# Wider weight blocks, and attention and the second layer nearer to their users, in a fused attention and two-layer kernel

## Chip, cores and metric

The kernel runs on one core of a Trainium2 chip. The metric is the time of one execution in microseconds (us) on the device; it is given as the median of several runs. One further execution was taken with the hardware profiler, and all rows of a profile below come from that one. TensorE is called PE in the profile, VectorE DVE, ScalarE ACT, GpSimd POOL and SyncE SP.

## What is computed

Pooled attention, and two feed-forward layers on its result, all in float32:

```python
def _attn_ref(q, kv, w_sr):                    # q: 1 x 12288 x 128, kv: 1 x 384 x 32 x 128
    kv_pool = kv.reshape(B, H // r, r, W // r, r, C).mean(axis=(2, 4))    # r = 4: 768 keys
    k = v = kv_pool.reshape(B, -1, C) @ w_sr
    s = (1.0 / np.sqrt(C)) * (q @ k.transpose(0, 2, 1))
    a = np.exp(s - s.max(-1, keepdims=True))
    a /= a.sum(-1, keepdims=True) + 1e-09
    return a @ v
def _moe_ref(x, w_in, w_out):                  # d_model 128, d_ff 2048
    h = x @ w_in
    return np.where(h > 0.0, h, np.exp(np.minimum(h, 0.0)) - 1.0) @ w_out
def _moe2_ref(x, w_in, w_out):
    h = x @ w_in
    return np.maximum(0.01 * h, h) @ w_out
# _moe2_ref(_moe_ref(attention of all 12288 rows))
```

Weights are handed in as 64-bit floats, as two 32-bit words each.

## The kernel before

**Tiling.** The 12288 rows are 24 chunks of 512. Every product is made of three matmuls on a high and a low part of each operand (`mm3`, lines 87 to 89), so that it keeps nearly float32 accuracy. Of a chunk, attention has four tiles of 128 rows (L347 to L426): scores against 768 keys into PSUM, the negated maximum on DVE (L351, `largest`), exp on ACT (L358), the inverse of the sum (L366, L367) and a scaling on POOL (L377). From chunk 2 on a tile is then sent through DRAM and fetched again in another order, transposed on DVE (L406, `turn`) and split into a high part on ACT (L422) and a low part on DVE (L426, the tail). Eighteen matmuls with v (L437, `values`) give the chunk's input of layer 1, split into xh on ACT (L441) and xl on DVE (L445).

**Units.** Of a chunk, each layer has 8 units, each of 256 of the 2048 hidden columns: 6 matmuls up into a PSUM place, the activation, and 6 matmuls down into the chunk's accumulator py. Layer 1's unit costs ACT two operations (L472, L475), DVE two (L479 and the tail L499) and POOL one (L485); layer 2's costs ACT two (L491, L495) and DVE one (L499). The output of layer 1 is split into x2h (ACT, L515) and x2l (DVE, L519), layer 2's input. The list `units` (L454 to L459) alternates a unit of layer 1 and one of layer 2, with layer 2 behind by D2 units of its kind: 12 units of layer 1 alone come first, and 12 of layer 2 alone come last. A unit's place in this list is its number n; the first unit is n = 0.

**Weights.** Each of the four matrices is brought in in blocks of WP = 256 hidden columns, 32 blocks in all. A block is loaded by SP into one of WS = 4 slots `ws` (L167). Then it is turned from 64-bit words into a high and a low float32 part (`w_parts`, L183): Abs of the upper words on ACT (L195), bounds on POOL (L199), on DVE a shift (L205), the sign (L212), the power (L219) and the lower words by that power (L229), on ACT the high part (L225); on PE three products with unit matrices, the rest (L236 to L238, of which the first, with a float32 operand, runs as two passes), and on ACT the low part (L241). The temporaries m, a and b of a block are one set out of two, held from Abs to the rest.

**Order.** A planner in the kernel's own text writes out the order of the instructions on every engine before the program runs (L535 to L807). Every `step` has an engine, an assumed length, the steps it follows and a key in units of n. Repeatedly the step is taken that can begin first by the assumed times; among those that can begin at once, the one with the lowest key. A step whose key is over 12 above the lowest open one is not yet looked at. `take` and `give` keep count of buffers: three PSUM places for scores, ups, rests and values together, the slots ws, the sets wt and others. On the chip each engine then runs its list in that order, and waits on semaphores where a real time differs from an assumed one.

The keys around the change: a chunk's attention from chunk 2 on starts at base = (n of its first layer-1 unit) - AHEAD, with 4 between its tiles; chunk 0 starts at -14 and chunk 1 at -8 with 2 between its tiles (L596). The maximum of a tile is at +0.5, its turn at +5.5, its tail at +6.5; with end the key of the last tile, values are at end + 7.5 and xl at end + 9.2. Layer 1's down of unit n is at n + 4, x2l at 0.4 behind the last down. A weight block is due 6 ahead of the first unit that uses it (L562, L563), and its load another 8 earlier. All ups keep the order of n (`chain["up"]`, L665).

Of the kernel before, what the change touches and what calls it, by code (L numbers as in the profile page):

```python
# [10 lines left out]
F32 = mybir.dt.float32  # L11
F32R = mybir.dt.float32r
U32 = mybir.dt.uint32
AF = mybir.ActivationFunctionType
# [4 lines left out]
P = 128  # L19
CH = 512  # L20
S = 32
WP = 256
WS = 4
D2 = 12
NEARLY = 2


LAG = {1: 4, 2: 4}
AHEAD = 28
SPACE = 4  # L30
WAHEAD = 6
REACH = 12
# [7 lines left out]
def pooled_attention_elu_leaky_kernel(  # L40
# [20 lines left out]
    nc = tc.nc  # L61
# [21 lines left out]
    def f(ap):  # L83
        return ap.bitcast(F32)
# [6 lines left out]
    def pool(name, bufs, **kw):  # L91
        return ctx.enter_context(tc.tile_pool(name=name, bufs=bufs, **kw))
# [25 lines left out]
    d_p = pool("scratch", 4, space=bass.MemoryType.DRAM)  # L118
    xs_p = pool("xs", 2)
    ws_p = pool("ws", WS)  # L120
    wt_p = pool("wt", 2)
    ps_p = [pool(f"ps_{i}", 1, space=PSUM) for i in range(3)]
    ps_y = pool("ps_y", 2, space=PSUM)

# [40 lines left out]
    wst, wt, w_ps = {}, {}, {}  # L165
# [17 lines left out]
    def w_parts(i):  # L183

        k, p = wjobs[i]
        pp, o = divmod(p * WP, CH)
        hi, lo = w_hi[k, pp][:, o:o + WP], w_lo[k, pp][:, o:o + WP]  # L190
        u = lambda x: x.bitcast(U32)

        def w_abs():
            wt[i] = [wt_p.tile([P, WP], t, tag=x, name=x) for x, t in zip("mab", (F32, F32, F32R))]
            nc.scalar.activation(out=wt[i][0], in_=f(wst[i][:, :, 1]), func=AF.Abs)  # L195

        def w_bound():
            m, a, b = wt[i]
            nc.gpsimd.tensor_scalar(  # L199
                out=m, in0=m, scalar1=TOP, scalar2=LEAST, op0=ALU.min, op1=ALU.max  # L200
            )

        def w_shift():
            m, a, b = wt[i]
            nc.vector.tensor_scalar(  # L205
                out=u(a), in0=u(m), scalar1=3, scalar2=0x3FFFFFF8,
                op0=ALU.logical_shift_left, op1=ALU.bitwise_and,
            )

        def w_sign():  # L210
            m, a, b = wt[i]
            nc.vector.scalar_tensor_tensor(  # L212
                out=u(a), in0=wst[i][:, :, 1], scalar=0xC0000000, in1=u(a),
                op0=ALU.bitwise_and, op1=ALU.bitwise_or,
            )

        def w_power():
            m, a, b = wt[i]
            nc.vector.tensor_scalar(  # L219
                out=u(m), in0=u(a), scalar1=0xFF800000, scalar2=None, op0=ALU.bitwise_and  # L220
            )

        def w_head():
            m, a, b = wt[i]
            nc.scalar.activation(out=hi, in_=a, func=AF.Copy)  # L225

        def w_b():
            m, a, b = wt[i]
            nc.vector.scalar_tensor_tensor(  # L229
                out=b, in0=wst[i][:, :, 0], scalar=2.0 ** -52, in1=m, op0=ALU.mult, op1=ALU.mult  # L230
            )

        def w_rest():
            m, a, b = wt[i]
            ps = w_ps[i][:, 0, :WP]
            nc.tensor.matmul(ps, ident, a, start=True, stop=False)  # L236
            nc.tensor.matmul(ps, minus, hi, start=False, stop=False)
            nc.tensor.matmul(ps, plus, b, start=False, stop=True)  # L238

        def w_tail():  # L240
            nc.scalar.activation(out=lo, in_=w_ps.pop(i)[:, 0, :WP], func=AF.Copy)  # L241

        return w_abs, w_bound, w_shift, w_sign, w_power, w_head, w_b, w_rest, w_tail

    with tc.tile_pool(name="kvp", bufs=1) as kvp, tc.tile_pool(name="sums", bufs=2) as sum_p:
# [7 lines left out]
        for i in range(WS):  # L255
# [9 lines left out]
            out=red,  # L265
            in_=ident.rearrange("p (h r w) -> p h w r", h=4, r=R),
# [4 lines left out]
            out=pool_m[:, 96:128],  # L271
# [231 lines left out]
    def down(n, i):  # L503
        m, c, u = units[n]
        if u == 0 and i == 0:
            yps[m, c] = ps_y.tile([P, CH], F32, tag="y", name="py")
        wh, wl = wblk(f"o{m}", 2 * u + i)
        mm3(
            yps[m, c], wh, wl, gh_u[n][:, i, :], gl_u[n][:, i, :],
            u == 0 and i == 0, u == NU - 1 and i == 1,  # L510
        )
# [26 lines left out]
    def step(engine, length, do, after, key):  # L538
        steps.append((engine, length, do, [a for a in after if a is not None], key))
        return len(steps) - 1  # L540

    def take(i, pool, n, bufs, put=None):

        takes.setdefault(i, []).append((pool, n, bufs, put))

    def give(i, pool, n):
        gives.setdefault(i, []).append((pool, n))

    PE, DVE, ACT, POOL, SP = range(5)
    where = {}  # L550
# [7 lines left out]
    w_ready = {}  # L558
    w_ends = []
    for i, (k, p) in enumerate(wjobs):  # L560
        m = int(k[1])
        n = where[m, 0, p] + (0 if k[0] == "i" else LAG[m])  # L562
        key = n - WAHEAD  # L563
        ld = None
        if i >= WS:
            ld = step(SP, 0.4, lambda i=i: load_w(i), [], key - 8)
            take(ld, "ws", i, WS)
        steps_w = w_parts(i)
        ab = step(ACT, 0.4, steps_w[0], [ld], key)
        bo = step(POOL, 0.5, steps_w[1], [ab], key)  # L570
        sh = step(DVE, 0.25, steps_w[2], [bo], key + 0.1)
        si = step(DVE, 0.4, steps_w[3], [sh], key + 0.2)
        po = step(DVE, 0.25, steps_w[4], [si], key + 0.3)
        hd = step(ACT, 0.4, steps_w[5], [si], key + 0.2)
        wb = step(DVE, 0.4, steps_w[6], [po], key + 0.4)
        wr = step(PE, 0.8, steps_w[7], [hd, wb], key + 0.5)
        take(wr, "ps", None, 3, lambda ps, i=i: w_ps.__setitem__(i, ps))
        wl = step(ACT, 0.45, steps_w[8], [wr], key + 0.6)
        give(wl, "ps", wr)
        take(ab, "wt", i, 2)  # L580
        give(wr, "wt", i)
        give(wb, "ws", i)
        w_ready[k, p] = wl


    x_ready = {}
# [7 lines left out]
    for c in range(NCH):  # L594
# [5 lines left out]
        for j in range(NJ):  # L600
            t = c * NJ + j
            key = base + gap * j
            after = [q_ready[c], last_sc]
# [34 lines left out]
        if c + 1 < NCH:  # L638
            ld = None
            if c + 1 >= 2:  # L640
                ld = step(SP, 2.2, lambda c=c: load_q(c + 1), [], end - 8)
# [20 lines left out]

    chain = dict.fromkeys(("up", "act", "tail", "down"))
    for n, (m, c, u) in enumerate(units):
        after = [w_ready[f"i{m}", u], x_ready[m, c], chain["up"]]  # L665
        u0 = step(PE, 0.69, lambda n=n: up(n, 0), after, n)
        u1 = chain["up"] = step(PE, 0.69, lambda n=n: up(n, 1), [u0], n)
        take(u0, "ps", None, 3, lambda ps, n=n: ps_u.__setitem__(n, ps))
        if m == 1:
            re = step(ACT, 0.95, lambda n=n: relu(n), [u1, chain["act"]], n + 0.5)  # L670
            xe = step(ACT, 1.05, lambda n=n: elu_exp(n), [re], n + 0.5)
            el = step(DVE, 1.3, lambda n=n: elu(n), [xe], n + 1)
            gh = step(POOL, 1.1, lambda n=n: elu_head(n), [el], n + 1.5)
            chain["act"] = re
            take(re, "r", n, 2)
            give(el, "r", n)
            take(el, "g", n, 3)
            take(gh, "gh", n, 4)
            give(el, "ps", u0)
            both = [el, gh]  # L680
        else:
            lh = step(ACT, 0.95, lambda n=n: leaky_head(n), [u1, chain["act"]], n + 0.5)
            lk = step(ACT, 0.95, lambda n=n: leaky(n), [lh], n + 0.5)
            chain["act"] = lk
            take(lh, "gh", n, 4)
            take(lk, "g", n, 3)
            give(lk, "ps", u0)
            both = [lh, lk]
        tl = chain["tail"] = step(DVE, 1.25, lambda n=n: tail(n), [*both, chain["tail"]], n + 2)
        take(tl, "gl", n, 3)  # L690
        give(tl, "g", n)
        d0 = step(
            PE, 0.69, lambda n=n: down(n, 0), [tl, w_ready[f"o{m}", u], chain["down"]],
            n + LAG[m],
        )
        d1 = chain["down"] = step(PE, 0.69, lambda n=n: down(n, 1), [d0], n + LAG[m])
        if u == 0:
            take(d0, "py", (m, c), 2)
        give(d1, "gl", n)
        give(d1, "gh", n)  # L700
        if u == NU - 1 and m == 1:
            hx = step(ACT, 0.55, lambda c=c: head_x2(c), [d1], n + LAG[m] + 0.3)
            x_ready[2, c] = step(DVE, 0.72, lambda c=c: tail_x2(c), [hx], n + LAG[m] + 0.4)
            take(hx, "x2", c, 2)
            give(x_ready[2, c], "py", (m, c))
        elif u == NU - 1:
            ty = step(DVE, 0.75, lambda c=c: turn_y(c), [d1], n + LAG[m] + 2)
            take(ty, "y", c, 1)
            give(ty, "py", (m, c))
            st = step(SP, 2.2, lambda c=c: store(c), [ty], n + LAG[m] + 3)  # L710
            give(st, "y", c)
        if u == NU - 1:
            give(u1, "xs" if m == 1 else "x2", c)
# [124 lines left out]
```

## Time and profile before

| | |
|---|---|
| median of 3 runs | 1362.68 us (1359.66 to 1364.47) |
| the profiled execution | 1353.33 us |
| its span, first to last instruction | 1351.5 us |
| busy: PE, DVE, ACT, POOL | 97%, 82%, 74%, 29% of the span |
| mean granted clock of TensorE | 0.994 of full speed |

Busy time of PE is modelled: matmuls overlap, and one of 512 columns shows about 0.39 us while the next one starts 0.23 us later. A PE that is busy all the time is therefore not proof of full use, but a PE that is idle is proof of a loss. The clock is given as a share of 2.4 GHz; it has two levels, 1.2 and 2.4 GHz, so that a mean of 0.85 says that 30% of the stretch ran at the lower one.

### The profile page before, as it was taken

What the parts mean: (1) busy time and instruction counts of PE and PEld (TensorE: products, weight loads), DVE (VectorE), ACT (ScalarE), POOL (GpSimd) and SP (SyncE); (2) the same over time, 40 slices, a digit from 0 to 9 for tenths busy, and PEclk for the clock granted to TensorE, in tenths of its full rate; (3) what the DMA queues carried; (4) which work ended last, traced back from release to release, by engine and by line L of the source; (5) the groups of instructions that cost most, each with busy time, mean ns of one, the idle gap of its engine ahead of it and who ended that gap; (6) DMA issues with size and microseconds to landing.
All of it is one profiled execution on the core that took longest, in us unless ns stands there. A gap on an engine that the chain in (4) does not pass through costs nothing.

```text
span 1351.5 us, 16631 instructions
## 1 busy us (share of the span) xinstructions
PE 1311.3 (97%) x5864; PEld 1085.9 (80%) x5864; DVE 1114.8 (82%) x1335; ACT 1000.0 (74%) x1245; POOL 385.7 (29%) x326
## 2 busy tenths in 40 slices
PE   5788999999999999999999999999999999999998
PEld 5576778888888888888888888888888888888886
DVE  6889998898887887887887888978878878887664
ACT  2666877778777786787777777777877867777775
POOL 0344432332332332322323323222323323231110
PEclk8999999999999999999999999999999999999999
DMA  8133322312322223223223123122222232220001
GB/s 250 56 109 118 113 63 73 81 54 69 82 67 64 79 62 79 70 64 86 70 63 86 59 63 86 59 63 80 65 75 72 61 87 71 55 78 24 8 8 16
DMA packets 170659, 97.63 MB, mean 72 GB/s; under 512 B 104912, under 2 KB 154192, under 8 KB 170576
## 3 DMA queue, kind: packets, MB, share of 16 engines
q1 hardware_dynamic: 169376, 96.36, 25.5%
q8 instruction: 47, 0.77, 0.2%
q10 hardware_dynamic: 1200, 0.20, 0.1%
q14 instruction: 36, 0.29, 0.1%
HBM read 55.64 MB, written 40.89 MB: 71 GB/s over the span
## 4 chain that ended last, share of the span: by engine, by line
PE 89%; DVE 6%; ACT 2%; issue 1%; POOL 1%; DMA 0%; SPq 0%; DVEq 0%; POOLq 0%; ACTq 0%
PE ps L88 15%; PE ps L87 15%; PE ps L89 15%; PE py L88 12%; PE py L89 12%; PE py L87 12%; PE ps L437 6%; DVE gl L499 1%; DVE a L212 1%; DVE g L479 1%; DVE el L426 1%; PE ps L236 1%; DVE nm L351 1%; DVE a L205 0%; DVE e L406 0%
## 5 line engine op out<-in xcount | busy, mean ns | idle before, releaser
L499 DVE TENSOR_TENSOR gl<-g,gh 128x1024 fp32r<-128x1024 f32 x384 | 470.2, 1253 | 94.5 <-POOL gh L485 76.8
L485 POOL TENSOR_SCALAR gh<-g 128x1024 fp32r<-128x1024 f32 x192 | 222.8, 1160 | 668.6 <-DVE g L479 632.4
L88 PE MATMUL py<-gl,wh_o 128*128 128x512 f32 x768 | 302.3, 394 | 2.3 <-DVE gl L499 2.2
L89 PE MATMUL py<-gh,wl_o 128*128 128x512 f32 x768 | 301.1, 392 | 0.0
L87 PE MATMUL py<-gh,wh_o 128*128 128x512 f32 x768 | 299.9, 390 | 0.2 <-DVE x2l L519 0.2
L472 ACT ACTIVATE r<-ps 128x1024 f32<-128x1024 f32 x192 | 197.0, 1026 | 138.7 <-PE ps L89 138.5
L479 DVE SCALAR_TENSOR_TENSOR g<-r,ps 128x1024 f32<-128x1024 f32 x192 | 232.9, 1213 | 72.7 <-ACT r L475 72.3
L491 ACT ACTIVATE gh<-ps 128x1024 fp32r<-128x1024 f32 x192 | 196.5, 1023 | 58.3 <-PE ps L89 58.3
L475 ACT ACTIVATE r<-r 128x1024 f32<-128x1024 f32 x192 | 203.8, 1062 | 5.8
L495 ACT ACTIVATE g<-ps 128x1024 f32<-128x1024 f32 x192 | 196.0, 1021 | 0.0
L377 POOL TENSOR_SCALAR e<-e,rs 128x768 f32<-128x768 f32 x88 | 135.3, 1538 | 172.7 <-DVE rs L367 127.8
L88 PEld LDWEIGHTS py<-gl,wh_o 128*128 128x128 f32 x768 | 144.2, 188 | 32.4 <-DVE gl L499 4.5
L89 PEld LDWEIGHTS py<-gh,wl_o 128*128 128x128 f32 x768 | 144.3, 188 | 30.6
L87 PEld LDWEIGHTS py<-gh,wh_o 128*128 128x128 f32 x768 | 144.3, 188 | 29.1 <-issue 0.4
L87 PE MATMUL ps<-xh,wh_i 128*128 128x512 f32 x384 | 151.1, 393 | 1.0 <-ACT e L358 1.0
L88 PE MATMUL ps<-xl,wh_i 128*128 128x512 f32 x384 | 151.6, 395 | 0.0
L89 PE MATMUL ps<-xh,wl_i 128*128 128x512 f32 x384 | 151.0, 393 | 0.0
L88 PE MATMUL ps<-x2l,wh_i 128*128 128x512 f32 x384 | 150.7, 392 | 0.0
L89 PE MATMUL ps<-x2h,wl_i 128*128 128x512 f32 x384 | 150.3, 391 | 0.0
L87 PE MATMUL ps<-x2h,wh_i 128*128 128x512 f32 x384 | 150.0, 391 | 0.0
L358 ACT ACTIVATE e<-ps,nm 128x768 f32<-128x768 f32 x96 | 85.9, 895 | 33.4 <-DVE nm L351 31.1
L426 DVE TENSOR_TENSOR el<-e,eh 128x768 fp32r<-128x768 f32 x88 | 99.1, 1126 | 7.5 <-ACT eh L422 7.4
(80 smaller groups left out, 1628.4 us busy)
## 6 DMA issues: line engine op xcount, KB each, us to landing
d<-e SPq DMA_DIRECT2D x88, 384.0 KB, 2.6
x<-d SPq DMA_DIRECT2D x88, 384.0 KB, 3.0
qn<-in_q_dram SPq DMA_DIRECT2D x96, 64.0 KB, 2.4
kv<-in_kv_dram SPq DMA_DIRECT2D x12, 512.0 KB, 8.7
out_dram<-y SPq DMA_DIRECT2D x94, 64.0 KB, 2.2
ws<-in_moe_w_in_dram SPq DMA_DIRECT2D x16, 256.0 KB, 2.9
ws<-in_moe_w_out_dram SPq DMA_DIRECT2D x16, 256.0 KB, 2.7
out_dram<-y ACTq DMA_DIRECT2D x2, 64.0 KB, 2.9
```

What stands on the lines that cost most here:

```text
L87: nc.tensor.matmul(ps, w_hi, x_hi, start=start, stop=False)
L88: nc.tensor.matmul(ps, w_hi, x_lo, start=False, stop=False)
L89: nc.tensor.matmul(ps, w_lo, x_hi, start=False, stop=stop)
L377: nc.gpsimd.tensor_scalar(out=x, in0=e, scalar1=rs_t.pop(t), scalar2=1.0, op0=ALU.mult, op1=ALU.mult)
L426: nc.vector.tensor_tensor(out=lo, in0=e_t.pop(t), in1=f(hi), op=ALU.subtract)
L472: nc.scalar.activation(out=r_u[n], in_=ps_u[n], func=AF.Relu, scale=-1.0)
L475: nc.scalar.activation(out=r_u[n], in_=r_u[n], func=AF.Exp, scale=-1.0)
L479: nc.vector.scalar_tensor_tensor(out=g_u[n], in0=r_u.pop(n), scalar=-1.0, in1=ps_u.pop(n), op0=ALU.add, op1=ALU.max)
L485: nc.gpsimd.tensor_scalar(out=gh_u[n], in0=g_u[n], scalar1=1.0, scalar2=0.0, op0=ALU.mult, op1=ALU.add)
L491: nc.scalar.activation(out=gh_u[n], in_=ps_u[n], func=AF.Prelu, alpha=0.01)
L495: nc.scalar.activation(out=g_u[n], in_=ps_u.pop(n), func=AF.Prelu, alpha=0.01)
L499: nc.vector.tensor_tensor(out=gl_u[n], in0=g_u.pop(n), in1=f(gh_u[n]), op=ALU.subtract)
```

## The change

Weight blocks become 512 columns wide, so there are 16 of them, in two slots for four. The temporaries m, a and b become three buffers of their own, one of each, taken and given back one by one: m from Abs to the last DVE step, a from the shift to the rest, b from that last DVE step to the rest. The assumed lengths of the weights' steps grow. Attention from chunk 2 on starts 24 units ahead of its chunk, in place of 28, and layer 2 runs 10 units behind layer 1, in place of 12. A block is due by the first unit that uses any of its columns. The diff, without the lines that only unpack m, a and b differently:

```diff
-WP = 256
-WS = 4
-D2 = 12
+WP = 512
+WS = 2
+D2 = 10
...
-AHEAD = 28
+AHEAD = 24
...
-    wt_p = pool("wt", 2)
+    wt_p = pool("wt", 1)
...
         def w_abs():
-            wt[i] = [wt_p.tile([P, WP], t, tag=x, name=x) for x, t in zip("mab", (F32, F32, F32R))]
-            nc.scalar.activation(out=wt[i][0], in_=f(wst[i][:, :, 1]), func=AF.Abs)
+            wt[i] = {"m": wt_p.tile([P, WP], F32, tag="m", name="m")}
+            nc.scalar.activation(out=wt[i]["m"], in_=f(wst[i][:, :, 1]), func=AF.Abs)
...
         def w_shift():
-            m, a, b = wt[i]
+            m, a = wt[i]["m"], wt_p.tile([P, WP], F32, tag="a", name="a")
+            wt[i]["a"] = a
...
         def w_b():
-            m, a, b = wt[i]
+            m, b = wt[i]["m"], wt_p.tile([P, WP], F32R, tag="b", name="b")
+            wt[i]["b"] = b
...
-        n = where[m, 0, p] + (0 if k[0] == "i" else LAG[m])
+        n = where[m, 0, p * WP // (2 * P)] + (0 if k[0] == "i" else LAG[m])
...
-        ab = step(ACT, 0.4, steps_w[0], [ld], key)
-        bo = step(POOL, 0.5, steps_w[1], [ab], key)
-        sh = step(DVE, 0.25, steps_w[2], [bo], key + 0.1)
-        si = step(DVE, 0.4, steps_w[3], [sh], key + 0.2)
-        po = step(DVE, 0.25, steps_w[4], [si], key + 0.3)
-        hd = step(ACT, 0.4, steps_w[5], [si], key + 0.2)
-        wb = step(DVE, 0.4, steps_w[6], [po], key + 0.4)
-        wr = step(PE, 0.8, steps_w[7], [hd, wb], key + 0.5)
+        ab = step(ACT, 0.65, steps_w[0], [ld], key)
+        bo = step(POOL, 1.0, steps_w[1], [ab], key)
+        sh = step(DVE, 0.6, steps_w[2], [bo], key + 0.1)
+        si = step(DVE, 0.7, steps_w[3], [sh], key + 0.2)
+        po = step(DVE, 0.6, steps_w[4], [si], key + 0.3)
+        hd = step(ACT, 0.65, steps_w[5], [si], key + 0.2)
+        wb = step(DVE, 0.7, steps_w[6], [po], key + 0.4)
+        wr = step(PE, 0.9, steps_w[7], [hd, wb], key + 0.5)
         take(wr, "ps", None, 3, lambda ps, i=i: w_ps.__setitem__(i, ps))
-        wl = step(ACT, 0.45, steps_w[8], [wr], key + 0.6)
+        wl = step(ACT, 0.65, steps_w[8], [wr], key + 0.6)
         give(wl, "ps", wr)
-        take(ab, "wt", i, 2)
-        give(wr, "wt", i)
+        for tag, begun, over in (("m", ab, wb), ("a", sh, wr), ("b", wb, wr)):
+            take(begun, tag, i, 1)
+            give(over, tag, i)
...
-        after = [w_ready[f"i{m}", u], x_ready[m, c], chain["up"]]
+        after = [w_ready[f"i{m}", 2 * P * u // WP], x_ready[m, c], chain["up"]]
...
-            PE, 0.69, lambda n=n: down(n, 0), [tl, w_ready[f"o{m}", u], chain["down"]],
+            PE, 0.69, lambda n=n: down(n, 0), [tl, w_ready[f"o{m}", 2 * P * u // WP], chain["down"]],
```

## Rows read from the trace of the kernel before

**Rows 1.** The page: busy us of each engine (share of the span), instructions.
```profile
PE 1311.3 (97%) x5864; PEld 1085.9 (80%) x5864; DVE 1114.8 (82%) x1335; ACT 1000.0 (74%) x1245; POOL 385.7 (29%) x326
```
**Rows 2.** Windows: stretch, length, busy PE, PEld, DVE, ACT, POOL; clock, DMA share, GB/s.
```profile
30.00:66.50 36.50, 26.80 (x148) 22.33 (x148) 32.83 (x73) 23.47 (x51) 11.93 (x16) 1.00 0.21 59
66.50:90.00 23.50, 19.39 (x76) 15.26 (x76) 18.38 (x31) 15.64 (x27) 10.60 (x12) 0.85 0.34 112
90.00:112.50 22.50, 19.42 (x91) 15.38 (x90) 21.75 (x37) 15.28 (x29) 7.46 (x9) 1.00 0.44 122
112.50:130.00 17.50, 14.98 (x65) 11.59 (x64) 17.26 (x23) 13.52 (x20) 10.29 (x8) 1.00 0.31 99
130.00:200.00 70.00, 68.66 (x312) 55.52 (x311) 68.48 (x112) 54.54 (x91) 30.28 (x26) 1.00 0.28 87
252.00:304.00 52.00, 52.00 (x234) 43.35 (x233) 43.84 (x50) 39.74 (x48) 15.31 (x12) 1.00 0.26 70
```
**Rows 3.** Groups, whole span: instruction xcount | busy us, mean ns | idle before, releasers.
```profile
L377 POOL TENSOR_SCALAR e<-e,rs 128x768 f32<-128x768 f32 x88 | 135.3, 1538 | 172.7 <-DVE rs L367 127.8 <-ACT x2h L515 37.5 <-issue 2.4
...
L212 DVE SCALAR_TENSOR_TENSOR a<-ws,a 128x256 uint32<-128x256 uint32 x32 | 19.2, 612 | 0.7
...
L229 DVE SCALAR_TENSOR_TENSOR b<-ws,m 128x256 fp32r<-128x256 uint32 x32 | 13.6, 440 | 2.0 <-DVE m L219 0.5
...
L205 DVE TENSOR_SCALAR a<-m 128x256 uint32<-128x256 uint32 x32 | 11.1, 360 | 3.2 <-POOL m L199 2.8 <-PE ps L238 0.5
...
L219 DVE TENSOR_SCALAR m<-a 128x256 uint32<-128x256 uint32 x32 | 10.1, 330 | 0.6
...
L284 DVE TENSOR_TENSOR s<-kv 128x512 f32<-128x512 f32 x12 | 8.3, 689 | 5.8 <-DMA kv<-in_kv_dram 5.4
```
**Rows 4.** Single lines: duration ns min/median/max, first and last start us, shape.
```profile
L212 DVE SCALAR_TENSOR_TENSOR a<-ws,a x32: 409/426/1267, 36.2 to 186.6; 128x256 uint32<-128x256 uint32 x32
...
L205 DVE TENSOR_SCALAR a<-m x32: 250/286/1157, 30.8 to 186.2; 128x256 uint32<-128x256 uint32 x32
```
**Rows 5.** PE in order of time: start, us, instruction [idle before]; up to unit 0.
```profile
64.91 0.70 PE L236 MATMUL ps<-a,ident 128*128 128x256 f32 x2 [2.30 <-ACT e L358]
...
66.57 0.63 PE L87 MATMUL ps<-xh,wh_i 128*128 128x512 f32 x1
```
**Rows 6.** DVE and PE in order of time, around units 8 and 11.
```profile
111.40 0.68 DVE L445 TENSOR_TENSOR xl<-ps,xh 128x512 fp32r<-128x512 f32 x1
...
112.48 0.40 PE L87 MATMUL ps<-xh,wh_i 128*128 128x512 f32 x1
...
124.74 0.40 PE L87 MATMUL ps<-xh,wh_i 128*128 128x512 f32 x1
...
131.52 0.68 DVE L519 TENSOR_TENSOR x2l<-py,x2h 128x512 fp32r<-128x512 f32 x1
```
**Rows 7.** Groups of DVE from 66.5 to 112.5 us.
```profile
L212 DVE SCALAR_TENSOR_TENSOR a<-ws,a 128x256 uint32<-128x256 uint32 x10 | 6.4, 636 | 0.3
...
L406 DVE STREAM_TRANSPOSE e<-x 128x768 f32<-128x768 f32 x3 | 2.9, 971 | 0.0
...
L426 DVE TENSOR_TENSOR el<-e,eh 128x768 fp32r<-128x768 f32 x3 | 2.9, 952 | 0.1
```
**Rows 8.** DVE and PE in order of time: chunk 8's xl, x2l and first readers.
```profile
460.07 0.69 DVE L445 TENSOR_TENSOR xl<-ps,xh 128x512 fp32r<-128x512 f32 x1 [1.05 <-ACT xh L441]
...
483.35 0.39 PE L87 MATMUL ps<-xh,wh_i 128*128 128x512 f32 x1
...
544.86 0.68 DVE L519 TENSOR_TENSOR x2l<-py,x2h 128x512 fp32r<-128x512 f32 x1
...
566.74 0.39 PE L87 MATMUL ps<-x2h,wh_i 128*128 128x512 f32 x1
```
**Rows 9.** DVE and PE in order of time: the last chunk's x2l and first reader.
```profile
1316.23 0.68 DVE L519 TENSOR_TENSOR x2l<-py,x2h 128x512 fp32r<-128x512 f32 x1
...
1319.79 0.39 PE L87 MATMUL ps<-x2h,wh_i 128*128 128x512 f32 x1
```

More of the change, by code (lines that the diff above doesn't have):

```diff
@@ L193, in w_abs @@
         def w_abs():
-            wt[i] = [wt_p.tile([P, WP], t, tag=x, name=x) for x, t in zip("mab", (F32, F32, F32R))]
-            nc.scalar.activation(out=wt[i][0], in_=f(wst[i][:, :, 1]), func=AF.Abs)
+            wt[i] = {"m": wt_p.tile([P, WP], F32, tag="m", name="m")}
+            nc.scalar.activation(out=wt[i]["m"], in_=f(wst[i][:, :, 1]), func=AF.Abs)
         def w_bound():
-            m, a, b = wt[i]
+            m = wt[i]["m"]
             nc.gpsimd.tensor_scalar(
@@ L210, in w_sign @@
         def w_sign():
-            m, a, b = wt[i]
+            m, a = wt[i]["m"], wt[i]["a"]
             nc.vector.scalar_tensor_tensor(
@@ L217, in w_power @@
         def w_power():
-            m, a, b = wt[i]
+            m, a = wt[i]["m"], wt[i]["a"]
             nc.vector.tensor_scalar(
@@ L223, in w_head @@
         def w_head():
-            m, a, b = wt[i]
+            a = wt[i]["a"]
             nc.scalar.activation(out=hi, in_=a, func=AF.Copy)
         def w_b():
-            m, a, b = wt[i]
+            m, b = wt[i]["m"], wt_p.tile([P, WP], F32R, tag="b", name="b")
+            wt[i]["b"] = b
             nc.vector.scalar_tensor_tensor(
@@ L233, in w_rest @@
         def w_rest():
-            m, a, b = wt[i]
+            a, b = wt[i]["a"], wt[i]["b"]
             ps = w_ps[i][:, 0, :WP]
```

## The prediction

> **What bounds the kernel now.** I read the page's busy times first, then the windows by stretch, then the groups of DVE, and last single instructions in order of time. PE is busy for 97% of the span [rows 1], but that is a mean over two regimes. Later on (252 to 304 us) PE fills its 52 us completely at the full clock, and DVE has 8.2 us of 52 to spare [rows 2]: there a step taken from DVE or ACT is worth nothing. The other regime is the fill, 30 to 200 us. In its five stretches PE stands idle for 9.7, 4.1, 3.1, 2.5 and 1.3 us (length less PE's busy time), 20.7 us in all, and from 66.5 to 90 the mean granted clock is 0.85, which costs 0.15 x 23.5 = 3.5 us more [rows 2]. So about 24 us is all that a reordering of the fill can win, since PE's own work stays. In the same stretches DVE is busy for 32.8 of 36.5, 18.4 of 23.5, 21.8 of 22.5, 17.3 of 17.5 and 68.5 of 70 us: from 90 us on DVE sets the pace; from 66.5 to 90 it has 5 us free, and chains through several engines do.
>
> **Wider weight blocks.** Of each block DVE runs four operations. Their totals are 19.2, 13.6, 11.1 and 10.1 us, 54.0 us in 32 blocks, 1.69 a block [rows 3]. Sixteen blocks of 512 columns take their place. The two-input operations, 0.426 us undisturbed (median of L212 [rows 4]), go to the 0.689 us of L284, which has two inputs of 512 columns [rows 3]. For the two TENSOR_SCALARs no row has 512 columns. They take 0.286 us for 256 (median of L205 [rows 4]), so at 512 between that and twice that, 0.57; I take 0.42, the middle, since columns cost them less than the two-input ones. A block then costs 2 x 0.69 + 2 x 0.42 = 2.2 us undisturbed.
>
> The second unknown is what a disturbed one costs. L212 has a median of 426 ns and a longest of 1267 [rows 4] at a mean of 612 [rows 3], so some of the 32 wait for something. An undisturbed narrow block is 2 x 0.426 + 2 x 0.286 = 1.42 us, so 0.27 us a block is such waiting; after the change it is between 0.27 (as much per instruction) and 0.54 (as much per column). I take 0.3: 2.5 us a block, 40 us in all, and DVE has 14 us less to do over the whole fill. The bounds are 6 us (0.57 and 0.54) and 18 us (0.286 and 0.27).
> The Trainium skill (SBUF — State Buffer, section Who interferes with whom) says that a VectorE instruction with two SBUF inputs and a reading GpSimd instruction exclude each other for a whole instruction, whichever began first. By that the wait is what is left of POOL's instruction, however wide DVE's own is, and the sum would be the one with 0.27; a mean of 1538 ns for POOL's L377 beside the longest L212 of 1267 [rows 3, 4] agrees.
>
> ACT's three operations a block shrink likewise, but ACT is busy for only 54.5 of 70 us and less before [rows 2], so I cost that at nothing; its own idle time hides it. PE's rests: two narrow ones took 1.66 us from the first one's start to the first unit's [rows 5], and one wide one streams the same columns: nothing. The loads move the same bytes, in 16 transfers for 32 and through two slots for four. They lie on SP's queue with the sends and fetches of attention, whose result has over 20 us to spare now (below). The four loads ahead of the loop become two of twice the size; the weights' first step on DVE comes only at 31 us and the first unit at 66.6 [rows 4, 5], so that is free too, and without that cover would cost one transfer's time.
>
> **Attention later.** A chunk's keys start 24 units ahead of its first unit, and D2 = 10 puts chunk 2's first unit at 22 for 20. So chunk 2's four score tiles get keys -2, 2, 6, 10 for -8, -4, 0, 4. Two of them now go ahead of the first unit. PE's last wait there, 2.30 us for the exp of one of them, goes: -2.3 us (bounds 0, if a rest waits for something else, and -4.0, if half of the slow clock behind it goes too, 1.7 of 3.5) [rows 2, 5]. The first unit then starts near 64.
>
> From the first unit to the ninth (66.6 to 112.5) the limit is chunk 1's xl: it ends at 112.1, and the ninth unit's first matmul starts at 112.5 [rows 6]. xl has key 7.2 (end -2 and 9.2), and DVE work with a lower key goes first. By keys, 9 wide blocks stand before it where 17 narrow ones did; in this stretch there were 9.5 narrow ones (L212 has 10, [rows 7]), and 5 wide ones will be: 9.5 x 1.69 - 5 x 2.5 = 3.6 us less. Of attention it had three turns and three tails, 2.9 us each [rows 7]. One tile of chunk 2 gets as far by key 7.2, so two of each go, 3.9 us, and a maximum comes in, no longer than a tail, 0.95: 2.9 us less. Together that is 6.5 us of DVE. From 90 to 112.5 DVE is busy 97%, and a saved us is a us; from 66.5 to 90 it is busy 78% [rows 2]. I take three quarters: -4.9 us (bounds 0 and -6.5). One score tile that PE had done by then, about 1 us, moves behind the ninth unit into a stretch with little idle: +1.0 us (bounds 0 and 2).
>
> From 112.5 to 200 PE is idle for 3.8 us [rows 2]. Seven wide blocks for fifteen narrow ones are 7.9 us less for DVE, against attention that comes later: -1 us (bounds 0 and -3).
>
> In the steady part the cover shrinks but lasts. A chunk's xl ends at 460.8 and is read at 483.4, 22.6 us later; its layer 2 starts 25 units on, at 566.7, so a unit is 3.34 us [rows 8], and four units less leave 9.2 us. Nothing that stands behind attention on DVE, ACT or SP is due before xl. Nothing; if that cover went, every chunk would pay.
>
> **The second layer two units earlier.** In the steady part layer 2 of a chunk starts 2 x D2 - 13 units after the end of its layer 1: 7 for 11. x2l ends at 545.5 and is read at 566.7, 21.2 us later [rows 8]; less 13.4 leaves 7.8: nothing. At the start layer 2's first unit becomes the twelfth, in place of the fourteenth. Now x2l of chunk 0 runs from 131.5 to 132.2 while the twelfth unit starts at 124.7 [rows 6]: 7.5 us too late as things stand. But DVE has less to do before it: 20 x 1.69 - 11 x 2.5 = 6.3 us of weights, two tiles of chunk 2 with their maximum, turn and tail (some 5.7 us, by [rows 7]) and the two operations of one unit, near 2.4 us: 14.4 us in all, so x2l ends near 118, and the twelfth unit, 6.2 us earlier by the terms above, comes at 118.5. I take 0 (bounds 0 and +7.5). At the end, x2l of the last chunk is ready 2.9 us before its reader [rows 9], with five units of layer 2 between it and layer 1's last up; there will be three. The last down can move up, since fewer units stand ahead of it: +0.5 us (bounds 0 and +2).
>
> **The sum.** -2.3 - 4.9 + 1.0 - 1.0 + 0 + 0.5 = -6.7 us. The profiled execution took 1353.33 us (span 1351.5 and 1.8 around it) and would take 1346.6. The median of the runs shown, 1362.68, is 9.35 us above it, so there it is 1356. A difference under 0.3%, 4 us, can't be told from none for this kernel.
>
> **The rivals.**
> - One set of temporaries holds the blocks up. The shift of a block can't start before the rest of the block ahead has run on PE, and its Abs not before that block's last DVE step. With two sets one such wait of the shift shows, 0.5 us [rows 3]. Unit work queued on DVE behind the shift waits too, and PE for that. At 0.8 us, half of what two narrow rests take, for the nine blocks ahead of the ninth unit it is 7 us, all of the gain: 1363. For it speaks DVE's full load; against it, that ten narrow blocks were spread over 46 us, so a wide one has some 9 us, more than its own 2.5 of DVE and 1.7 of PE. Chance 0.22.
> The Trainium skill (Trainium Kernel Development and Optimization, section Best Practices) asks for double buffers so that DMA and compute overlap, which speaks against single ones in general; no run here shows yet what they cost.
> - The slower one: layer 2's first up meets its x2l in DVE's backlog, and, since all ups keep one order, the layer-1 units behind it wait as well. Place: the twelfth unit. Price: 7.5 us with the backlog as it is, of which PE fills 2.3 with work that the earlier first unit released, and 0.5 at the end: +5.7 us, 1368. It ends above the time before if DVE's work ahead of x2l shrinks by less than 5.7 us, not 14.4. For it: DVE is busy for 17.3 of the 17.5 us before 130 [rows 2]. Against it: x2l's key, 11.4, is below those of the units that follow. Chance 0.16.
> - The whole saving counts, and half the slow clock goes: -4.0 - 6.5 - 3.0 + 1.0 = -12.5 us: 1350. Chance 0.12.
> - My forecast, 1352 to 1358: 0.50.
>
> **How the numbers follow.** Faster by over 0.3%: forecast and whole saving, 0.62. Same: 0.22. Slower: 0.16. The range runs from the whole saving, less the 3 us by which the lowest run lies under the median, to two thirds of the way into the slower rival: 1347 to 1366.
>
> **What would show it.** The first matmul on xh near 64, with no wait of 2 us for an exp before it; the ninth unit near 105; L205 and L212 16 times, at 0.4 and 0.7 us; PE idle for under 16 us between 30 and 200; xl some 9 us ahead of its reader in the steady part and no idle there; x2l of chunk 0 near 118. Wrong would be: DVE's shift waiting for PE's rests, PE waiting for x2l at the twelfth unit, or any wait of PE after 200 us.

## The result, and the profile after

| | before | after |
|---|---|---|
| median of the executions taken with the prediction | 1363.58 us (4, from 1359.66 to 1364.91) | 1347.76 us (4, from 1346.46 to 1349.57) |
| ratio, 95% interval | | 0.9903 (0.9876 to 0.9929) |
| the profiled execution | 1353.33 us | 1346.46 us |
| its span | 1351.5 us | 1344.5 us |

The changed kernel is faster by about 1%; the forecast was 1356 in a range from 1347 to 1366. The two comparisons don't agree: by the medians the gain is 15.8 us, by the two profiled executions 6.9 us, and the forecast had 6.7. Most of what follows is about that gap.

The windows of after, in the stretches of [rows 2] and with the same columns (stretch, length, busy time and instructions of PE, PEld, DVE, ACT and POOL, clock, DMA):

```profile
30.00:66.50 36.50, 27.40 (x138) 20.99 (x138) 29.55 (x54) 24.10 (x41) 12.56 (x13) 1.00 0.20 51
66.50:90.00 23.50, 20.13 (x74) 14.37 (x75) 21.81 (x32) 17.04 (x26) 9.68 (x9) 0.93 0.50 157
90.00:112.50 22.50, 21.23 (x88) 15.64 (x87) 20.24 (x25) 15.72 (x22) 9.08 (x8) 1.00 0.35 106
112.50:130.00 17.50, 15.40 (x61) 10.49 (x61) 17.07 (x22) 10.53 (x15) 7.07 (x5) 1.00 0.24 56
130.00:200.00 70.00, 67.94 (x290) 53.82 (x289) 63.14 (x77) 56.69 (x73) 23.10 (x19) 1.00 0.30 85
252.00:304.00 52.00, 52.00 (x234) 43.39 (x233) 43.87 (x50) 39.73 (x48) 14.99 (x13) 1.00 0.27 71
```

PE is idle for 9.1, 3.4, 1.3, 2.1 and 2.1 us: 17.9 us in the fill, where it was 20.7. The lower clock takes 0.07 x 23.5 = 1.6 us for 3.5. DVE is less full from 90 us on, 20.2 of 22.5 for 21.8 and 63.1 of 70 for 68.5. Later PE is as full as before.

The four operations of the weights on DVE, as groups (busy us, mean ns, idle before), beside [rows 3]:

```profile
L213 DVE SCALAR_TENSOR_TENSOR a<-ws,a 128x512 uint32<-128x512 uint32 x16 | 15.0, 939 | 0.5
...
L231 DVE SCALAR_TENSOR_TENSOR b<-ws,m 128x512 fp32r<-128x512 uint32 x16 | 11.5, 718 | 1.7 <-DVE m L220 0.5
...
L206 DVE TENSOR_SCALAR a<-m 128x512 uint32<-128x512 uint32 x16 | 8.8, 549 | 2.1 <-PE ps L238 1.6 <-POOL m L199 0.5
...
L220 DVE TENSOR_SCALAR m<-a 128x512 uint32<-128x512 uint32 x16 | 7.4, 463 | 0.5
```

Together 42.7 us for 54.0. And the two lines by themselves (min/median/max ns), beside [rows 4]:

```profile
L206 DVE TENSOR_SCALAR a<-m x16: 406/424/1303, 36.4 to 165.3; 128x512 uint32<-128x512 uint32 x16
...
L213 DVE SCALAR_TENSOR_TENSOR a<-ws,a x16: 671/693/1416, 36.9 to 165.7; 128x512 uint32<-128x512 uint32 x16
```

PE in order of time at the first unit, at the rest that follows it, at the ninth unit and at the twelfth, which is layer 2's first, beside [rows 5, 6]:

```profile
57.56 0.50 PE L87 MATMUL ps<-xh,wh_i 128*128 128x512 f32 x1
...
68.89 1.12 PE L238 MATMUL ps<-a,ident 128*128 128x512 f32 x2 [2.97 <-ACT e L360]
...
104.20 0.39 PE L87 MATMUL ps<-xh,wh_i 128*128 128x512 f32 x1
...
123.69 0.40 PE L87 MATMUL ps<-x2h,wh_i 128*128 128x512 f32 x1
```

The first unit starts 9.0 us earlier, at 57.6; the ninth 8.3 us earlier, at 104.2; the twelfth only 1.0 us earlier, at 123.7. The wait for an exp that stood ahead of the first unit has not gone: it is 2.97 us long and now stands ahead of a rest behind the second unit.

### The profile page after: what moved, and what is told of

Read it like the earlier page. It is cut to its first block, busy times and chain, and to the rows that moved or that the text cites. A ratio compares the mean times of both kernels' runs of the same rounds, so it can differ in the third digit from the quotient of the medians.

```text
span 1344.5 us, 16194 instructions
## 1 busy us (share of the span) xinstructions
PE 1307.3 (97%) x5800; PEld 1077.7 (80%) x5800; DVE 1106.1 (82%) x1271; ACT 994.2 (74%) x1197; POOL 377.0 (28%) x310
## 4 chain that ended last, share of the span: by engine, by line
PE 92%; DVE 4%; ACT 1%; issue 1%; DMA 1%; SPq 0%; POOL 0%; DVEq 0%; POOLq 0%
PE ps L88 15%; PE ps L87 15%; PE ps L89 15%; PE py L88 13%; PE py L87 13%; PE py L89 13%; PE ps L439 7%; DVE gl L501 1%; PE ps L238 1%; DMA kv<-in_kv_dram 1%; DVE g L481 1%; DVE a L213 1%; DVE a L206 0%; DVE nm L353 0%; ACT e L360 0%
## 5 line engine op out<-in xcount | busy, mean ns | idle before, releaser
L487 POOL TENSOR_SCALAR gh<-g 128x1024 fp32r<-128x1024 f32 x192 | 216.1, 1126 | 674.5 <-DVE g L481 654.1
L428 DVE TENSOR_TENSOR el<-e,eh 128x768 fp32r<-128x768 f32 x88 | 100.0, 1137 | 19.5 <-ACT eh L424 19.4
```

Of the source, the lines that this page charges most:

```text
L428: nc.vector.tensor_tensor(out=lo, in0=e_t.pop(t), in1=f(hi), op=ALU.subtract)
L487: nc.gpsimd.tensor_scalar(out=gh_u[n], in0=g_u[n], scalar1=1.0, scalar2=0.0, op0=ALU.mult, op1=ALU.add)
```

## The experiments

### The three parts, one by one and in pairs

The change has three parts: the wide blocks with their temporaries, AHEAD, and D2. With all of them and none of them that makes eight kernels. Each part alone is one of these edits:

```diff
-WP = 256                       # wide: with all that the diff does to the weights
-WS = 4
+WP = 512
+WS = 2
...
-AHEAD = 28                     # ahead
+AHEAD = 24
...
-D2 = 12                        # d2
+D2 = 10
```

Wide alone: 

> Wide blocks and their three single temporaries alone; attention 28 ahead and layer 2 12 behind, as before. Theory A (the gain is DVE work taken out of the fill): DVE's four weight operations fall from 54.0 us to about 40, the ninth unit starts some 3 us earlier than at 112.5, and the time falls by 4 to 6 us, a ratio near 0.996. Rival B (the gain is that attention of chunk 2 no longer stands ahead of the first unit): the first unit stays at 66 to 67 us and the time within 2 us of before.

Ahead alone: 

> Attention 24 units ahead alone; narrow blocks, layer 2 12 behind. Theory A: the wait of 2.3 us before the first unit goes, the ninth unit gains 2 to 3 us more, and the time falls by 3 to 4 us, a ratio near 0.997. Rival B: the first unit starts near 58 us and the time falls by most of the 15.8 us that the whole change gained, a ratio of 0.990 to 0.993.

D2 alone: 

> Layer 2 10 units behind alone; narrow blocks, attention 28 ahead of a chunk that starts two units later (so its keys in the fill move by 2 of the 6). Theory A: the twelfth unit waits for x2l of chunk 0, PE loses up to 4 us there, and the time is between 2 us less and 4 us more than before. Rival B: the two tiles of chunk 2 move by 2 keys only, to -6 and -2, still ahead of the first unit: no change within 2 us. A third theory C (layer 2's units, which need half the DVE time, come earlier and fill PE): 3 to 6 us less.

Ahead and D2, with narrow blocks: 

> Attention 24 ahead and layer 2 10 behind, with narrow blocks: the whole change but the weights. Theory A: 3 to 5 us less than before, the rest of the change's gain belonging to the wide blocks. Rival B: as fast as the whole change, a ratio of 0.990 to 0.992. If the sum of the parts is below the whole, they work together.

Wide and ahead: 

> Wide blocks and attention 24 ahead, layer 2 still 12 behind. Theory P (the steady part's loss hangs on AHEAD and D2 alone, by where attention's steps fall between the units): PE loses about 10 us after 200 us, as with 24 and 12 and narrow blocks (waits of 0.2 us, twice every two chunks), and the time is near 1358 to 1362. Theory F (only the fill matters): the fill gains as in the whole change, and the time is near 1350.

Wide and D2: 

> Wide blocks and layer 2 10 behind, attention still 28 ahead. Theory P: PE's first down of a chunk waits for x2l every second chunk, 7 to 8 us after 200 us, as with 28 and 10 and narrow blocks, and the time is 1360 to 1368. Theory F: near 1350.

Measured, as ratios to the kernel before on the same chip (95% interval); the other columns are of each one's trace. PE's idle time in the fill is 170 us less its busy time from 30 to 200; in the steady part 1120 less that from 200 to 1320:

| kernel | AHEAD, D2 | ratio | first unit | ninth unit | PE idle, fill | PE idle, steady |
|---|---|---|---|---|---|---|
| before | 28, 12 | 1 | 66.6 | 112.5 | 20.7 | 0.2 |
| wide | 28, 12 | 1.0047 (1.0017 to 1.0077) | 59.2 | 116.3 | 21.6 | 0.0 |
| ahead | 24, 12 | 1.0003 (0.9982 to 1.0025) | 66.4 | 110.0 | 19.4 | 3.7 |
| d2 | 28, 10 | 1.0050 (1.0028 to 1.0073) | 64.9 | 108.8 | 22.7 | 4.2 |
| wide, ahead | 24, 12 | 0.9991 (0.9979 to 1.0003) | 58.6 | 106.1 | 20.4 | 3.2 |
| wide, d2 | 28, 10 | 0.9996 (0.9983 to 1.0008) | 58.3 | 106.7 | 20.6 | 4.0 |
| ahead, d2 | 24, 10 | 0.9948 (0.9928 to 0.9969) | 65.1 | 110.2 | 19.6 | 1.2 |
| all: after | 24, 10 | 0.9903 (0.9876 to 0.9929) | 57.6 | 104.2 | 17.9 | 0.0 |

No part alone is a gain, and two of them alone are a loss. Their single effects add up to 0.0047 + 0.0003 + 0.0050, 1% slower, where together they are 1% faster. Theory A, which gave wide blocks alone 4 to 6 us, fell; so did B, which gave the gain to AHEAD, and F, by which only the fill counts. For D2 alone none of the three theories came out: it was slower by 5.3 us, above the 4 that was the most any of them allowed. AHEAD and D2 together gained 6.4 us, more than the 3 to 5 of theory A and less than B wanted. Theory P held: the steady part's loss goes with AHEAD and D2 and hardly with the blocks.

What PE waits for from 200 to 1320 us (waits in total, times, longest), in d2:

```profile
PE py L87 <- DVE x2l L519: 4.2, 10, 0.5
```

In ahead:

```profile
PE ps L87 <- DVE g L479: 2.0, 10, 0.2
PE ps L437 <- ACT g L495: 1.7, 10, 0.2
```

With D2 = 10 alone, every second chunk's first down waits for py to be read out by x2l. With AHEAD = 24 alone, an up and a chunk's values wait, every second chunk, for a PSUM place that an earlier unit still holds. Both are short, but a wait costs more than its idle time, since PE's overlap of matmuls starts anew: in ahead the up that waits 0.20 us starts 0.60 us after the matmul ahead of it, and the next one 0.31 us later, where two steps are 0.46 us else. So every second chunk takes 53.27 us in place of 52.27, 1.0 us for 0.4 us of waits. With both edits these waits don't recur: ahead with d2 has three in all, 1.2 us, and after has no wait of PE in this stretch. None of them is the wait of an up for xl or x2l, whose cover the prediction had weighed; what counts is where attention's steps fall between the units, and who holds a place or a buffer just then.

Wide alone shows what single temporaries can do. PE from 94 to 110 us, in order of time, in the kernel with wide blocks alone:

```profile
95.24 2.04 PE L238 MATMUL ps<-a,ident 128*128 128x512 f32 x2 [3.09 <-DVE g L481]
...
105.57 2.08 PE L238 MATMUL ps<-a,ident 128*128 128x512 f32 x2 [3.49 <-ACT e L360]
```

And DVE just behind the first of them:

```profile
97.32 0.43 DVE L206 TENSOR_SCALAR a<-m 128x512 uint32<-128x512 uint32 x1 [1.63 <-PE ps L238]
```

A rest waits for a PSUM place held by a unit or an attention tile, and DVE's shift of the next block waits for that rest. Twice the granted clock falls to 1.2 GHz about such a wait, as the rest's 2.04 us beside the 1.12 us of the rest in after shows. From 90 to 112.5 us the mean granted clock is 0.70, which costs 0.30 x 22.5 = 6.8 us. The first unit is early, at 59.2, and the ninth is 4 us later than before.

### The kernel before, once more

> The kernel before itself, for a second trace of it: its times lay between 1352 and 1374 us, and the profiled execution, 1353.3, was at the low end. Theory D (its slower executions lose their time in the fill, through a late transfer that changes nothing in the order): span near 1360 with 8 us more of PE's idle time before 200 us and none after. Theory E (they lose it in the steady part, each chunk a little): PE waits after 200 us that sum to 5 us or more.

This execution took 1362.32 us, 9 us more than the first one of the same kernel, and close to that kernel's median. Neither theory was right in its sums: PE's idle time is 18.8 us in the fill and 0.05 us from 200 to 1320. The time is lost in two ways that are no idle time. A part of it is lost in the fill, at the lower clock. The mean granted clock of the fill's first three stretches is 0.90, 0.85 and 0.92, where it was 1.00, 0.85 and 1.00, and the first unit starts at 69.4 us for 66.6. The first stretch, in the second trace:

```profile
30.00:66.50 36.50, 28.44 (x140) 24.40 (x140) 31.24 (x65) 21.52 (x47) 10.53 (x14) 0.90 0.20 53
```

The larger part is lost later. Windows from 530 to 870 us, in the first trace of before:

```profile
530.00:870.00 340.00, 340.00 (x1521) 283.14 (x1520) 288.30 (x320) 261.13 (x308) 98.69 (x78) 1.00 0.25 69
```

In the second trace of the same kernel:

```profile
530.00:870.00 340.00, 340.00 (x1498) 280.67 (x1497) 282.62 (x312) 257.16 (x303) 97.06 (x77) 1.00 0.25 69
```

In after:

```profile
530.00:870.00 340.00, 340.00 (x1522) 283.72 (x1521) 286.36 (x319) 261.38 (x308) 98.36 (x78) 1.00 0.25 68
```

PE is busy all the time in all three, at the full clock, and yet does 1498 matmuls for 1521: 1.5% less. The cause is its rhythm. In the first trace a 512-column matmul starts 226, 229 or 232 ns after the one ahead of it, 229 on average; in the second, from 504 to 920 us, nearly every one starts 233.3 ns after, and a chunk takes 53.21 us for 52.3. PE of the second trace in order of time, where it changes:

```profile
502.76 0.39 PE L87 MATMUL py<-gh,wh_o 128*128 128x512 f32 x1
502.99 0.39 PE L88 MATMUL py<-gl,wh_o 128*128 128x512 f32 x1
503.22 0.42 PE L89 MATMUL py<-gh,wl_o 128*128 128x512 f32 x1
503.47 0.40 PE L87 MATMUL ps<-xh,wh_i 128*128 128x512 f32 x1
503.71 0.40 PE L88 MATMUL ps<-xl,wh_i 128*128 128x512 f32 x1
503.94 0.40 PE L89 MATMUL ps<-xh,wl_i 128*128 128x512 f32 x1
504.18 0.40 PE L87 MATMUL ps<-xh,wh_i 128*128 128x512 f32 x1
```

Two steps are late, 0.25 and 0.24 us for 0.23: the unit's first weights wait a moment for their PSUM place, which the exp of an attention tile gives back just then. From there on the steps are 0.233, through scores and values of eight chunks. Those chunks are 7.4 us longer than at the other rhythm; the first trace had 0.7 us of another disturbance in that part, and chunk 2's first up comes at 166.4 for 163.7, 2.7 us later: 7.4 - 0.7 + 2.7 = 9.4 us, against the 9.0 us between the two spans. In wide alone, the slower rhythm holds from 818 us to the end, begun by the same pair of late steps at the same place of a chunk. In d2 and in wide with d2 it holds for some 92 us at a time, in wide with ahead twice for 8 us. Where it begins, from 200 us on, the matmul is one whose weights wait for a semaphore, but that alone is not enough: in d2 and in wide with d2 no step there is later than 0.234 us, and the first trace of before has seven waits of such weight loads, 0.2 us at most, that begin nothing.

How much of the time goes which way can be read from the matmuls that are left at 200 us. Windows from 200 us to the end, for the first trace of before, its second one, after, and ahead with d2:

```profile
200.00:1351.50 1151.50, 1145.84 (x5109) 952.00 (x5107) 938.74 (x1025) 870.63 (x1009) 314.43 (x250) 1.00 0.24 64
...
200.00:1360.50 1160.50, 1155.00 (x5121) 956.35 (x5119) 942.13 (x1029) 872.12 (x1010) 315.38 (x251) 1.00 0.24 64
...
200.00:1344.50 1144.50, 1139.00 (x5083) 948.46 (x5081) 937.17 (x1026) 863.39 (x1004) 314.78 (x251) 1.00 0.25 65
...
200.00:1352.80 1152.80, 1146.10 (x5110) 953.42 (x5108) 943.50 (x1033) 868.00 (x1009) 318.76 (x252) 1.00 0.24 65
```

A matmul takes 0.224 us on average in the first trace. The second trace of before has 12 more of them left, 2.7 us, and loses the other 6.5 us by its pace. After has 26 fewer left than the first trace, 5.8 us won in the fill, and 38 fewer than the second one, 8.5 us; with 7.5 us of pace that makes the 16.0 us between those two spans, as much as the medians differ. Ahead with d2 has as many left as the first trace of before, and a span 1.3 us longer than that: by these traces its gain over before's median is none in the fill, and lies in what before's other executions lose.

### The changed kernel, once more

> The changed kernel itself once more, in more executions beside the kernel before. Theory S (the kernel before loses 0.9 us a chunk in a slower rhythm of PE's 512-column matmuls, 233.3 for 229 ns, into which a short wait of PE can throw it and which then lasts; the changed kernel has no wait of PE after 200 us): its times stay within 4 us of each other, near 1348, while before spreads over 10 us or more, and the trace has no stretch at 233 ns. Theory T (before's extra time is spent in the fill): the two spread alike.

Median 1348.70 (1345.24 to 1350.26), before beside it on the same chip 1366.64 (1357.72 to 1369.34): ratio 0.9871 (0.9840 to 0.9901). By the spread, 5.0 us (a little over the 4 that it said) against 11.6, theory S came out and theory T did not. In neither trace of after is there a stretch at 233 ns after 200 us; before, there are two, from 141 to 152 and from 160 to 167 us, which cost some 0.3 us by the same pace. The two traces of after agree to 1.1 us in span, and PE's idle time in the fill is 17.9 and 18.0 us. So the gain has two sources: about 7 us between the best traced execution of before and after, most of it in the fill, and 9 us that before loses in an execution near its median, 6 to 7 of them to the slower rhythm and about 3 in the fill, at the lower clock. That its other executions lose their time in the same two ways is likely by their times, but not shown: only two of them have a trace.

### The temporaries

> Attention 24 ahead, layer 2 10 behind, as in the changed kernel, and its three single temporaries taken and given back one by one, but blocks of 256 columns in four slots. With two sets and narrow blocks this order took 1356.0. Theory A (width saves DVE work): 1356 to 1360, the temporaries costing 0 to 4 us. Theory G (what the wide blocks bring is not DVE work but fewer rests and so fewer PSUM places and waits of PE): also 1356 or above. Theory H (the single temporaries, given back early, bring the gain): near 1348, as the whole change.

```diff
-WP = 512
-WS = 2
+WP = 256
+WS = 4
```

1365.93 us, ratio 1.0039 (1.0027 to 1.0051): ten microseconds above the same order of keys with two sets (1355.98 us, ratio 0.9948; not run beside each other, so the ratios to before are the better comparison, 0.9% apart). With narrow blocks single temporaries do cost: PE is idle for 25.8 us in the fill for 19.6. Theory H fell. In this kernel four rests stand ahead of the first unit and it starts at 60.4 too, so an early first unit needs no wide blocks, and is no gain by itself.

> The changed kernel with two buffers for the temporary a, so that a block's shift need not wait for the rest of the block ahead. Theory R (single temporaries hold the blocks up): the shift's waits for PE's rest, 1.6 us in 4 places, go, and the time falls by 2 to 5 us. Theory A: those waits are covered by PE's other work, and the time stays within 2 us of 1348. Theory U: 3 us or more to either side by another order.

```diff
+    wa_p = pool("wa", 2)
...
-            m, a = wt[i]["m"], wt_p.tile([P, WP], F32, tag="a", name="a")
+            m, a = wt[i]["m"], wa_p.tile([P, WP], F32, tag="a", name="a")
...
-            take(begun, tag, i, 1)
+            take(begun, tag, i, 2 if tag == "a" else 1)
```

Median 1348.91 us, beside after's 1348.70. DVE's waits from 28 to 200 us in this kernel have no line for the shift and PE any more, but this one:

```profile
DVE b L232 <- PE ps L241: 2.6, 3, 1.0
```

The wait moved on to b, which is still single. With wide blocks theory R fell, in time. One of its six executions took 1366.87 us, 18 us above the others; twenty chunks at 0.9 us would be as much, but it has no trace, so whether the slower rhythm can take hold with 24 and 10 as well is open. Two buffers for all three temporaries, with wide blocks, were not run.

### The order itself

> The changed kernel with the planner's assumed lengths of the wide steps set to the measured ones: Abs 0.61, bounds 0.75, shift and power 0.44, high part 0.62, rest 1.33, low part 0.58 us, for 0.65, 1.0, 0.6, 0.65, 0.9 and 0.65. Theory A (the fill is bound by DVE's work): same work, another order, within 2 us of 1348. Theory U (the order that the planner happens on matters as much as the work): 3 us or more to either side, all of it before 200 us.

1350.52 us (1347.75 to 1351.19), 0.9885 (0.9855 to 0.9915): 1.8 us above after, but 2.5 above the 1348 that theory A had named: a little outside it, and short of theory U's 3. PE is idle for 18.0 us in the fill, and for 1.2 us in the steady part, where after has none.

> The changed kernel with weight blocks due 7 units ahead for 6. PE's longest wait in the fill is now a rest that waits for the exp of an attention tile (4.1 us, twice). Theory U: with weights ahead of the attention tile that wait goes, 2 to 4 us less, if the new order makes no other. Theory A: DVE's work is the same, within 2 us of 1348.

1349.21 us, 0.9877 (0.9848 to 0.9906): the same as after. The longest wait of a rest for an exp is 2.1 us in place of 3.0, and downs that wait for gl took 5.7 us for 2.7: a wait went and another came. No kernel run was faster than after.

## Why the prediction was right, and where it was not

**The regimes.** Right: nothing was gained where PE is full, as far as work on DVE goes. Incomplete: that PE is busy at the full clock was read as "nothing to win", and in other executions than the one it read there are 0.9 us a chunk to win there, over eight chunks in the second trace, hidden from busy time, idle time and clock, and to be seen only in the count of matmuls per time.

**The cost of a block.** Right in kind. 0.42 and 0.69 us were taken, 0.424 and 0.693 are the medians. The waits beside them came to 42.7 / 16 - 2.23 = 0.44 us a block, inside the bounds 0.27 and 0.54 and above the 0.3 taken: DVE saves 11.3 us, not 14. (The lower bound of that saving comes to 5 us by its own terms, not 6.) A wait of 0.44 for 0.27 us a block lies nearer to a cost that grows with the operation's length than to one that does not.
The Trainium skill (SBUF — State Buffer, section Who interferes with whom) calls the port pair that DVE and POOL share an exclusive lock, by which a wait for POOL is what is left of POOL's instruction, and the waits per block would have stayed as they were. The trace agrees with that for the longest instruction alone: L213's lies 0.72 us above its median, where L212's lay 0.84 us above.

**The first unit.** The step that failed: it gave the first unit 2.3 us from attention and nothing from the width of the blocks. With AHEAD and D2 and narrow blocks the wait of 2.3 us for an exp does go, but two others come, 1.3 and 0.6 us, and the unit starts at 65.1, 1.5 us earlier. With AHEAD alone it starts at 66.4, and ten score tiles stand ahead of it as before. With the wide blocks and their single temporaries alone it starts at 59.2. What had stood ahead of it were the rests of seven narrow blocks, each with its PSUM place and its chain; two stand there now, and four with narrow blocks and single temporaries, where it starts at 60.4. In [rows 5] the rest that waits was in plain view, and the prediction looked at what it waited for and not at why it stood there.

**From the first to the ninth unit.** 46.6 us, where it was 45.9: nothing of the 4.9 us was gained here. The prediction counted five wide blocks on DVE in this stretch, and eight fall into it, since fewer stand ahead of the first unit:

```profile
L213 DVE SCALAR_TENSOR_TENSOR a<-ws,a x8: 685/693/1412, 57.6 to 103.0; 128x512 uint32<-128x512 uint32 x8
```

At 42.7 / 16 = 2.67 us that is 21.4 us of weights on DVE, where ten narrow ones at 1.69 took 16.9: more, not 3.6 us less. Chunk 1's xl, taken as the limit, ends at 101.3 and no longer sets the ninth unit; PE's longest wait of the fill now lies in this stretch. The two errors cancel, which is luck: 105 was forecast for the ninth unit, 104.2 came.

**The twelfth unit.** 118.5 was forecast, 123.7 came. x2l, forecast near 118, ends at 123.8, just when its reader needs it; PE had scores to do until then and did not wait for it, so the slower rival did not come about. Between the ninth and the twelfth unit PE now does 15 more matmuls of downs and 15 of scores than before, some 6 us of work, and that takes most of the 7.2 us by which the stretch is longer.

**The steady part and the end.** Right in outcome: xl stands 10.5 us ahead of its reader in chunk 8 (9.2 forecast) and x2l 6.8 us (7.8), with no wait. The reason given was not sufficient: with one of the two edits alone less of the cover goes, and yet PE lost 3.7 or 4.2 us of idle time, 7 to 10 us with restarts. The last chunk's x2l ends 0.8 us before its reader; that is the one place where nothing is left.

**The first rival.** Single temporaries held the blocks up with narrow blocks (10 us) and in wide alone. The sign that was named for it, DVE's shift waiting for a rest on PE, is there in after too, but it costs no time that two buffers for a could win back. DVE's waits from 28 to 200 us in after:

```profile
DVE a L206 <- PE ps L238: 1.6, 4, 0.7
```

**From the profile to the median.** The term that was mis-sized. The sum was -6.7 us for a profiled execution, and the two profiled executions differ by 6.9. Then 9.35 us were added to go over to the median, as if that were a constant of measuring. For after it is 1.3 us, and 3.5 in its second set of executions. It was a property of the kernel before, of which the profiled execution was one of the best: over 35 executions it went from 1352 to 1374 us. Had that distance, twice the spread of the three runs (4.8 us), been taken as a loss that the trace did not contain and that the change might remove, the likeliest time would have been 1353.33 - 6.7 = 1346.6 us, and a little above it for a median.

**The range.** The median lies 0.8 us above the lower end of the range, and not for the reason that this end had, the whole saving in the fill. Of the fill's 24 us, 2.8 us of idle time and 1.9 us of slow clock were won, 4.7 us (5.8 if the matmuls left at 200 us are counted); PE stays idle for 17.9 us there, not under 16. That the range held is in part luck: the rest came from a loss that the prediction did not know.

## What to carry to other kernels

Where the median lies well above the profiled execution, profile again before sizing a change: the distance may be a loss that the first trace does not contain, and a change may remove it. In a loop whose bound engine never idles, count its instructions per time in several traces, as busy time and clock can be the same for two speeds. Parts of a schedule are not additive: a shift that alone opens a wait every second turn of the loop may, with another shift, close it, so measure the combination and not only the parts.

## What was not expected of the hardware

PE's stream of 512-column matmuls with a weight load for each has two rhythms at the same full clock, 229 ns and 233.3 ns a matmul. The slower one held for 416 us in the second trace of before and for over 500 us in wide alone, through matmuls of other sizes. In both it set in with a weight load that came late, in steps of 255 and 241 ns for 229. Late steps don't always do that: the second trace of after has 16 steps of 240 ns from 200 us on and stays in the faster rhythm, and in d2 the slower one began without a late step. All begins that were seen from 200 us on lie at a matmul whose weights wait for a semaphore, as do many that begin nothing; the ends lie at or shortly ahead of a wait of PE, or at nothing that the trace shows, as at 920 us. Why there are two, what sets them, and why after has stayed in the faster one after 200 us, is open: no run set the rhythm on purpose.
